# ScalarE copies the first 256 output columns of each expert tile, and issues the second expert's weight loads

## Chip, core and metric

The kernel runs on one core of a Trainium2 chip. The metric is the time of one execution on the device, in microseconds (us). It was measured three times: 692.98, 693.09 and 696.32 us, median 693.09 us. Below, PE is TensorE, DVE is VectorE, ACT is ScalarE, POOL is GpSimd and SP is SyncE; PSUM is the memory of eight banks that matmuls write to, and SBUF is the main on-chip memory.

## What is computed

Two blocks follow one another. The first is causal attention with a window of 64 positions; the second is a mixture of experts in which every token goes to one of eight experts.

```python
# attention: q, k, v are (8 batches, 8 heads, 576 positions, 64)
scores = where(0 <= i - j < 64, q @ k.T / 8, -1e9);  attn = softmax(scores) @ v
x = attn.transpose(0, 2, 1, 3).reshape(4608, 512)
# experts: w1 is (8, 512, 1024), w2 is (8, 1024, 512)
e = argmax(x @ w_gate);  g = softmax(x @ w_gate)[e]
out[n] = g[n] * (relu(x[n] @ w1[e]) @ w2[e])
```

All data is 32-bit floating point. An fp32 matmul of the program stands as two records in the trace, which is why counts of matmuls in the profile are twice those in the code.

## The kernel before

**Stages.** Until about 200 us the attention runs, head pair by head pair; its rows, scaled with the gate, are stored to `x_dram`. Meanwhile the tokens are counted per expert, and a table of slots (`perm_i`) sorts them by expert. Then the experts run, in tiles of up to 256 tokens. The rows of a tile are gathered from `x_dram` by an indirect DMA of POOL (`gather`, L282), turned by sixteen 32x32-block transposes of DVE into `xn` (`turned_blocks`, L319), copied by two instructions of ACT into `xq` (`keep_turned`, L334), multiplied, and written to their places in `out` by two indirect DMAs of POOL (`scatter`, L300), first the half `ys[1]`, then the half `ys[0]`.

**Kinds of tile.** A whole tile (256 tokens) is done with a seven-product scheme of the Strassen kind: `hidden` (L345) makes relu(x w1) in seven products of 128x128 matmuls, and `output` (L402) multiplies by w2 in seven products of 128x256 matmuls, which collect in PSUM banks 4 (`yps[0]`, halves `yx` and `yx2`), 5 (`yw`, `yy2`), 7 (`yy`) and 2 (`yw2`). The scheme needs sums of weight blocks, which POOL forms (`sums_w1`, `sums_w2`, L152 and L155, four instructions each, all of them line L142 in the profile), and sums of token blocks, which DVE forms (`sums_x`, L338, and `left_sums`, L127). An expert's last tile, if it holds 160 tokens or fewer, is a half tile (`half_tile`, L445) and, with 96 or fewer, a rest tile (`rest_tile`, L492); these use plain products. In this run there are 16 whole tiles, 3 half tiles and 2 rest tiles (L353 has 1792 records and a whole tile has 112; L479 has 48 and a half tile 16; L530 has 64 and a rest tile 32).

**The end of a tile lies in the next one.** `finish` (L434) adds the last PSUM results into `ys[0]` and `ys[1]` with DVE. It is called at the start of the following tile's `body` (L545), together with `scatter` and, at the border of two experts, with the weight sums (`between`). The first two whole tiles, called `tile0` and `tile1` here, are written out before the loop over experts (L1063 to L1122); all later ones go through `expert` (L1142).

**Order of the work.** The whole kernel stands under `manual_schedule`: each engine executes its instructions in the order in which the program text issues them. Where a generator such as `hidden` or `output` stops at a `yield`, the caller can put other work. Three orders matter here:

- In `half_tile` ACT gets, in this order, the relu of the hidden values (L463), two copies of 32x128 blocks out of bank 5 (L483, c = 0 and 2; DVE has c = 1 and 3), and then `keep_turned`, which makes the next tile's input. PE gets the L474 products (32 tokens, into bank 5) and then the L479 products (128 tokens, all 512 columns of bank 4).
- In `output` PE ends with the products `yy`, `yy2`, `yw2` and `yx2`, in this order (L422 to L431). ACT has the copy of `yx` into `y1` (L411) after the first product and `keep_turned` after the third.
- SP issues the loads of the second expert's `w1` and `w2` (2 MB each, L1133 and L1134, seen as L159 and L162 in the profile) after everything of the first two tiles; as SP has nothing else to do, it runs ahead of the other engines. The weights of the experts after it are issued from ACT's queue within a whole tile of the expert before (L1147).

The memory for the second expert's weights and sums (pool `wp`) is taken after the attention's pools (`held`: `xsp`, `small`, `rp`, and the table `hi`) have been given back.

Of the kernel before, what the change touches and what calls it, by code (L numbers as in the profile page):

```python
# [36 lines left out]
def kernel(  # L37
# [10 lines left out]
    nc = tc.nc  # L48
    P = nc.NUM_PARTITIONS
    B, H, S, D = q.shape  # L50
    NT, DM = out.shape
# [21 lines left out]
    QD = 32  # L73
# [27 lines left out]
    w1_of = lambda pool, i: pool.tile([P, NG, FF], F32, name=f"w1_{i}")  # L101
    w2_of = lambda pool, i: pool.tile([P, FT, DM], F32, name=f"w2_{i}")
# [55 lines left out]
    def load_w1(e, queue=nc.sync):  # L158
        queue.dma_start(out=w1s[e % NW][:], in_=w1v[e])  # L159

    def load_w2(e, queue=nc.sync):
        queue.dma_start(out=w2s[e % NW][:], in_=w2v[e])  # L162
# [103 lines left out]
    hs = v_m(2080, 4, HF, P)  # L266
    u3 = v_m(4128, HF, P)
    y1, v1, v3 = (v_m(4640 + n * HM, HM) for n in range(3))
    v02 = v_m(4640 + 3 * HM, DM)
    v2 = v02[:, HM:]  # L270
    xn = v_m(1024, C, NG, P)
    at_g = consts.tile([P, C], I32, name="at_g")
    at_s = consts.tile([P, C], I32, name="at_s")
# [45 lines left out]
    def turned_blocks():  # L319

        rows = xg_all.rearrange("p c (g b j) -> p c g b j", b=P // QD, j=QD)
        for a in range(P // QD):
            for b in range(P // QD):
                V.transpose(  # L324
                    out=xn[b * QD : (b + 1) * QD, :, :, a * QD : (a + 1) * QD].rearrange("p c g i -> p (c g) i"),
                    in_=rows[a * QD : (a + 1) * QD, :, :, b, :].rearrange("p c g j -> p (c g) j"),
                )
                yield
# [66 lines left out]
    def product_y(acc, a, b, start=True, stop=True):  # L395
        for f in range(HF):
            nc.tensor.matmul(  # L397
                acc, lhsT=a[:, f, :], rhs=b[:, f, :],
                start=(start and f == 0), stop=(stop and f == HF - 1), skip_group_check=True,
            )  # L400

    def output(e, blocks=None, next_x=True):  # L402

        b11, b12, b21, b22 = w2q(e)
        t = s2s[e % NW]
        a11, a12, a21, a22 = hq[:, 0, 0], hq[:, 1, 0], hq[:, 0, 1], hq[:, 1, 1]
        form(left_sums(V, hs, a11, a12, a21, a22))
        if blocks is not None:
            form_all(blocks)
        product_y(yx, a11, b11)  # L410
        nc.scalar.copy(out=y1, in_=yx)  # L411
        yield
        product_y(yw, a22, t[:, 3])
        yield
        product_y(yx, a12, b21, start=False)
        if blocks is None:
            sums_x(tps)
        elif next_x:
            keep_turned()
            sums_x([xn[:, c] for c in range(C)])  # L420
        yield
        product_y(yy, hs[:, 1], t[:, 1])  # L422
        yield
        product_y(yy2, hs[:, 2], t[:, 2])
        plus(v1, yy, y1)
        plus(v3, yy2, v1)
        V.tensor_tensor(out=ys[1][:, lo_], in0=v3, in1=yw, op=ALU.subtract)
        yield
        product_y(yw2, hs[:, 0], t[:, 0])
        yield  # L430
        product_y(yx2, hs[:, 3], b22)  # L431
        yield

    def finish():  # L434

        plus(ys[1][:, hi_], yw2, v3)
        plus(v2, yw2, v1)
        plus(ys[0], yps[0], v02)

    hp = qk_m(8192, FT, HALF)  # L440
    pps = [banks[i](0, rows_, HALF) for i, rows_ in ((0, 3), (1, 3), (6, 2))]
# [3 lines left out]
    def half_tile(e, blocks, after, next_x):  # L445

        w1, w2 = w1s[e % NW], w2s[e % NW]
        f = 0
        for n, acc in enumerate(pps):
            f0 = f  # L450
            for i in range(acc.shape[1]):
                for g in range(NG):
                    nc.tensor.matmul(
                        acc[:, i], lhsT=w1[:, g, f * P : (f + 1) * P],
                        rhs=xq[:, g].rearrange("p c s -> p (c s)")[:, 0:HALF],
                        start=(i + g == 0), stop=(g == NG - 1), skip_group_check=True,
                    )
                f += 1
            if n == 1:
                some(blocks, 8)  # L460
                V.tensor_scalar_max(hp[:, f0:f], acc, 0.0)
            else:
                relu(out=hp[:, f0:f], in_=acc)  # L463
        V.memset(v1, 0.0)
        V.memset(yw2, 0.0)
        form_all(blocks)
        if after is not None:
            gather(perm_i[:, after])

        quad = lambda c: slice(c * QD, (c + 1) * QD)  # L470
        y = y2(0, P)
        for f in range(FT):
            for c in range(NQ):
                nc.tensor.matmul(  # L474
                    y[quad(c)], lhsT=hp[:, f, P:], rhs=w2[:, f, c * P : (c + 1) * P], start=(f == 0), stop=(f == FT - 1),
                    skip_group_check=True,
                )
        for f in range(FT):
            nc.tensor.matmul(yps[0], lhsT=hp[:, f, 0:P], rhs=w2[:, f, :], start=(f == 0), stop=(f == FT - 1))  # L479
        for c in range(NQ):  # L480
            copy = V.tensor_copy if c % 2 else nc.scalar.copy
            to = ys[1] if c < NQ // 2 else v3
            copy(out=to[0:QD, c % 2 * P : (c % 2 + 1) * P], in_=y[quad(c)])  # L483
        if next_x:
            keep_turned()
            sums_x([xn[:, c] for c in range(C)])
# [5 lines left out]
    def rest_tile(e, blocks, after, next_x):  # L492

        w1, w2 = w1s[e % NW], w2s[e % NW]

        def rows(acc, tokens, ways):
            n, width = P // ways, FF // ways
            for g in range(NG):
                for c in range(ways):
                    nc.tensor.matmul(  # L500
                        acc[c * n : (c + 1) * n, 0:width], lhsT=xq[:, g, 0, tokens],
                        rhs=w1[:, g, c * width : (c + 1) * width], start=(g == 0), stop=(g == NG - 1),
                        skip_group_check=True,
                    )

        a, b = banks[0](0, FF // 2), banks[1](0, FF // 4)
        rows(b, slice(L, L + QD), 4)
        relu(out=hr4, in_=b)
        rows(a, slice(0, L), 2)
        relu(out=hr, in_=a)  # L510
        for h, t, acc in ((hr4, ht4, banks[3](0, HF // 2, P)), (hr, ht, banks[6](0, HF, P))):
            for i in range(h.shape[1] // P):
                nc.tensor.transpose(out=acc[:, i], in_=h[:, i * P : (i + 1) * P], identity=ident[:])
            nc.scalar.copy(out=t.rearrange("p i c s -> p i (c s)"), in_=acc)
        V.memset(v1, 0.0)
        V.memset(yw2, 0.0)
        form_all(blocks)
        if after is not None:
            gather(perm_i[:, after])

        y, y4 = banks[7](0, DM), y2(0, P)
        for f in range(FT):
            for c in range(4):
                nc.tensor.matmul(
                    y4[c * QD : (c + 1) * QD], lhsT=ht4[:, f % (HF // 2), f // (HF // 2)],
                    rhs=w2[:, f, c * P : (c + 1) * P], start=(f == 0), stop=(f == FT - 1), skip_group_check=True,
                )
        for f in range(FT):
            for c in range(2):
                nc.tensor.matmul(  # L530
                    y[c * L : (c + 1) * L, c * HM : (c + 1) * HM], lhsT=ht[:, f % HF, f // HF],
                    rhs=w2[:, f, c * HM : (c + 1) * HM], start=(f == 0), stop=(f == FT - 1), skip_group_check=True,
                )
        for c in range(4):
            nc.scalar.copy(out=yps[0][L : L + QD, c * P : (c + 1) * P], in_=y4[c * QD : (c + 1) * QD])
        if next_x:
            keep_turned()
            sums_x([xn[:, c] for c in range(C)])
        nc.scalar.copy(out=yps[0][0:L, hi_], in_=y[L:, hi_])
        V.tensor_copy(out=yps[0][0:L, lo_], in_=y[0:L, lo_])  # L540

    def whole_tile():
        pass
# [20 lines left out]
            ahead()  # L564
        form_all(parts)

    with tc.manual_schedule(), ExitStack() as held, ExitStack() as brief:
        xsp = held.enter_context(tc.tile_pool(name="xsp", bufs=7))
        small = held.enter_context(tc.tile_pool(name="small", bufs=4))
        rp = held.enter_context(tc.tile_pool(name="rp", bufs=2))  # L570
# [538 lines left out]
            next(table, None)  # L1109
        assert next(tile0, None) is None  # L1110
        gather(perm_i[:, 3 * C : 4 * C])
        V.memset(v02[:, lo_], 0.0)
        finish()
        scatter(perm_e[:, 0:C])
        blocks = turned_blocks()
        tile1 = chain(hidden(0), output(0, blocks))
        for _ in range(8):
            next(tile1)
        regs, end, most = loads()
        gather(perm_i[:, 4 * C : 5 * C])  # L1120
        for _ in tile1:
            pass  # L1122

    wp = ctx.enter_context(tc.tile_pool(name="wp", bufs=1))

    w1s.append(w1_of(wp, 1))
    s1s.append(s1_of(wp, 1))
    w2s.append(w2_of(wp, 1))
    s2s.append(s2_of(wp, 1))


    with tc.manual_schedule():
        load_w1(1)  # L1133
        load_w2(1)  # L1134

        def at(n):
            n = nc.s_assert_within(
# [113 lines left out]
```

## Time and profile before

| what | value |
|---|---|
| three runs | 692.98, 693.09, 696.32 us; median 693.09 us |
| the profiled execution | 693.54 us |
| its span, first to last instruction | 691.8 us |
| granted clock of PE over the span | 0.999 of full speed |
| PE busy | 669.9 us (97%) |
| weight loads of PE busy | 590.7 us (85%) |
| DVE busy | 501.5 us (72%) |
| POOL busy | 357.4 us (52%) |
| ACT busy | 263.5 us (38%) |
| DMA queues | 94.52 MB, mean 137 GB/s |

The span is what the trace covers; the execution's own time is 1.7 us longer. "PE busy" counts a matmul from its start to its modelled end; consecutive matmuls overlap, so the interval from one to the next is shorter than a matmul's own duration. In the answers of the trace a line of a timeline gives the start in us, the duration in us, the engine, the line of the code, the operation, what it writes and reads, its shape and its count, and in brackets the idle time before it with what ended that. `ACTq`, `SPq` and `POOLq` are the sequencers of these engines, which issue DMAs.

### The profile page before, as it was taken

What the parts mean: (1) busy time and instruction counts of PE and PEld (TensorE: products, weight loads), DVE (VectorE), ACT (ScalarE), POOL (GpSimd) and SP (SyncE); (2) the same over time, 40 slices, a digit from 0 to 9 for tenths busy, and PEclk for the clock granted to TensorE, in tenths of its full rate; (3) what the DMA queues carried; (4) which work ended last, traced back from release to release, by engine and by line L of the source; (5) the groups of instructions that cost most, each with busy time, mean ns of one, the idle gap of its engine ahead of it and who ended that gap; (6) DMA issues with size and microseconds to landing.
All of it is one profiled execution on the core that took longest, in us unless ns stands there. A gap on an engine that the chain in (4) does not pass through costs nothing. (4 is left out here: it accounts for less than half of the span.)

```text
span 691.8 us, 18001 instructions
## 1 busy us (share of the span) xinstructions
PE 669.9 (97%) x6894; PEld 590.7 (85%) x6894; DVE 501.5 (72%) x1646; ACT 263.5 (38%) x662; POOL 357.4 (52%) x364
## 2 busy tenths in 40 slices
PE   6999999999999999999999999999999999999996
PEld 4888888888788897997899899899689799689995
DVE  3677998898967678766776686586867486766864
ACT  5889888888855011111111121121121121121211
POOL 6414649478852208766452357356265757264012
PEclk9999999999999999999999999999999999999999
DMA  9997789988435351622601161171135161111021
GB/s 213 217 223 177 180 186 241 215 200 211 182 109 168 126 180 64 242 113 73 256 29 63 60 243 63 63 259 48 64 134 212 50 243 63 65 39 63 2 63 62
DMA packets 136767, 94.52 MB, mean 137 GB/s; under 512 B 115567, under 2 KB 115583, under 8 KB 136640
## 3 DMA queue, kind: packets, MB, share of 16 engines
q1 hardware_dynamic: 114944, 38.29, 22.2%
q0 software_dynamic: 8544, 26.50, 11.8%
q10 hardware_dynamic: 13152, 28.05, 11.6%
q8 instruction: 78, 1.28, 0.7%
q14 instruction: 49, 0.40, 0.2%
HBM read 73.94 MB, written 20.45 MB: 136 GB/s over the span
## 5 line engine op out<-in xcount | busy, mean ns | idle before, releaser
L324 DVE STREAM_TRANSPOSE v_m<-qk_m 32x256 f32<-32x256 f32 x320 | 139.3, 435 | 6.9 <-DMA qk_m<-x_dram,at_g 0.9
L285 POOL DMA_INDIRECT qk_m<-x_dram,at_g x42 | 45.4, 1080 | 164.2 <-DVE v_m L324 154.1
L353 PE MATMUL bank<-qk_m,s 128*128 128x128 f32 x1024 | 122.4, 275 | 0.0
L353 PEld LDWEIGHTS bank<-qk_m,s 128*128 128x128 f32 x1024 | 118.3, 192 | 0.0
L723 ACT ACTIVATE pr<-pr,mx 128x128 f32<-128x128 f32 x288 | 89.6, 390 | 22.0 <-DVE mx L713 21.5
L353 PE MATMUL bank<-qk_m,w 128*128 128x128 f32 x768 | 94.1, 276 | 1.0 <-PEq L1156 0.5
L353 PEld LDWEIGHTS bank<-qk_m,w 128*128 128x128 f32 x768 | 90.3, 192 | 4.7 <-issue 4.4
L713 DVE CUSTOM_DVE_ANT_0 pr<-bank,mask 128x128 f32<-128x128 f32 x288 | 64.4, 286 | 20.5 <-PE bank L700 17.7
L393 DVE TENSOR_TENSOR v_m<-bank,v_m 128x256 f32<-128x256 f32 (+1 forms) x95 | 43.8, 479 | 38.2 <-PE bank L397 27.3
L304 POOL DMA_INDIRECT out_dram<-v_m,at_s x42 | 42.5, 1011 | 54.7 <-DVE v_m L393 50.5
L142 POOL TENSOR_TENSOR s<-w 128x1024 f32<-128x1024 f32 x22 | 52.2, 2373 | 0.0
L641 POOL COPY v_m<-v_m 64x520 f32<-64x520 f32 x32 | 20.1, 627 | 61.3 <-DMA v_m<-in_v_dram 52.2
L746 PEld LDWEIGHTS bank<-v_m,pT 128*64 128x64 f32 x1152 | 40.7, 137 | 11.4 <-issue 3.9
L746 PE MATMUL bank<-v_m,pT 128*64 128x65 f32 x1152 | 47.9, 227 | 2.1 <-POOL v_m L645 0.8
L397 PE MATMUL bank<-qkT_m,v_m 128*128 128x256 f32 x216 | 48.3, 379 | 0.0
L360 ACT COPY qk_m<-bank 128x512 f32<-128x512 f32 x16 | 9.4, 587 | 99.8 <-PE bank L353 73.7
L336 ACT COPY qk_m<-v_m 128x512 f32<-128x512 f32 x40 | 22.7, 615 | 61.4 <-DVE v_m L324 61.4
L397 PEld LDWEIGHTS bank<-qkT_m,v_m 128*128 128x128 f32 x216 | 41.0, 190 | 5.5
L700 PE MATMUL bank<-qkT_m 64*64 64x128 f32 x1152 | 43.6, 281 | 0.7 <-DVE mx L713 0.7
L886 POOL TENSOR_SCALAR xs<-xs,gate 128x512 f32<-128x512 f32 x27 | 42.0, 1566 | 2.2 <-DVE gate L846 1.5
L731 PE MATMUL bank<-ident,pr 128*128 128x128 f32 x288 | 42.0, 282 | 0.0
L363 DVE TENSOR_TENSOR qk_m<-bank,qk_m 128x512 f32<-128x512 f32 x16 | 11.1, 692 | 40.7 <-PE bank L353 40.7
(197 smaller groups left out, 1247.4 us busy)
## 6 DMA issues: line engine op xcount, KB each, us to landing
w<-in_moe_w_dram ACTq DMA_DIRECT2D x9, 2048.0 KB, 8.9
qk_m<-in_q_dram SPq DMA_DIRECT2D x72, 128.0 KB, 3.5
qk_m<-in_k_dram SPq DMA_DIRECT2D x66, 128.0 KB, 3.6
v_m<-in_v_dram SPq DMA_DIRECT2D x64, 128.0 KB, 3.4
qk_m<-in_moe_w_dram ACTq DMA_DIRECT2D x3, 2048.0 KB, 11.1
w<-in_moe_w_dram SPq DMA_DIRECT2D x2, 2048.0 KB, 14.0
w<-in_moe_w_dram ACTq DMA_DIRECT2D x4, 512.0 KB, 5.0
x_dram<-xs POOLq DMA_DIRECT2D x4, 512.0 KB, 4.9
```

Of the source, the lines that this page charges most:

```text
L142: op()
L285: G.indirect_dma_start(out=xg[c], out_offset=None, in_=x_dram[:, :], in_offset=bass.IndirectOffsetOnAxis(ap=at_g[:, c : c + 1], axis=0),)
L304: put = G.indirect_dma_start(out=out[:, :], out_offset=bass.IndirectOffsetOnAxis(ap=at_s[:, c : c + 1], axis=0), in_=ys[c], in_offset=None ...
L324: V.transpose(out=xn[b * QD : (b + 1) * QD, :, :, a * QD : (a + 1) * QD].rearrange("p c g i -> p (c g) i"), in_=rows[a * QD : (a + 1) * QD ...
L353: nc.tensor.matmul(acc[:, f, :], lhsT=a[:, g, f * P : (f + 1) * P], rhs=b[:, g, :], start=(first and f == 0 and g == 0), stop=(g == HG - 1 ...
L393: plus = lambda out, a, b: V.tensor_tensor(out=out, in0=a, in1=b, op=ALU.add)
L397: nc.tensor.matmul(acc, lhsT=a[:, f, :], rhs=b[:, f, :], start=(start and f == 0), stop=(stop and f == HF - 1), skip_group_check=True,)
L700: nc.tensor.matmul(out_, lhsT=qT[rows, t, a * WINDOW : (a + 1) * WINDOW], rhs=rhs, start=True, stop=True, skip_group_check=True,)
L713: V.tensor_tensor_reduce(out=prs[h][:, m, :], in0=scs[h][:, m, :], in1=mask[:, m0 + m, :], scale=-scale, scalar=-2 * MASKED, op0=ALU.add, ...
L723: nc.scalar.activation(out=y, in_=y, func=AF.Exp, scale=-1.0, bias=mx[:, h, m : m + 1])
L731: nc.tensor.transpose(out=tr[:, m, :], in_=prs[h][:, m, :], identity=ident[:])
L746: nc.tensor.matmul(px[a * D : (a + 1) * D, h, m, :], lhsT=pTs[h][:, m, a * D : (a + 1) * D], rhs=vt[:, h, :], start=True, stop=True, skip_ ...
```

## The change

ACT, not DVE, now moves the first 256 columns of the first 128 tokens from PSUM to `ys[0]`: in `output` after the product `yy` has been issued, in `half_tile` after the L479 products. `finish` adds only the other 256 columns; `v2` no longer needs a zeroed half beside it, and the memset at L1112 goes. In `rest_tile` the copies that went to the first half of bank 4 go to `ys[0]` instead. The memory of the attention's pools is given back before `tile1`, and ACT's queue issues the loads of `w1` and `w2` of expert 1 within `tile1`, after the third and the fifth step of `hidden`; SP's two loads go.

```diff
     y1, v1, v3 = (v_m(4640 + n * HM, HM) for n in range(3))
-    v02 = v_m(4640 + 3 * HM, DM)
-    v2 = v02[:, HM:]
+    v2 = v_m(4640 + 3 * HM, HM)
...
         product_y(yy, hs[:, 1], t[:, 1])
+        nc.scalar.copy(out=ys[0][:, lo_], in_=yx)
         yield
         product_y(yy2, hs[:, 2], t[:, 2])
...
         plus(v2, yw2, v1)
-        plus(ys[0], yps[0], v02)
+        plus(ys[0][:, hi_], yx2, v2)
...
         for f in range(FT):
             nc.tensor.matmul(yps[0], lhsT=hp[:, f, 0:P], rhs=w2[:, f, :], start=(f == 0), stop=(f == FT - 1))
+        nc.scalar.copy(out=ys[0][:, lo_], in_=yx)
         for c in range(NQ):
             copy = V.tensor_copy if c % 2 else nc.scalar.copy
...
         for c in range(4):
-            nc.scalar.copy(out=yps[0][L : L + QD, c * P : (c + 1) * P], in_=y4[c * QD : (c + 1) * QD])
+            to = (ys if c < 2 else yps)[0]
+            nc.scalar.copy(out=to[L : L + QD, c * P : (c + 1) * P], in_=y4[c * QD : (c + 1) * QD])
...
         nc.scalar.copy(out=yps[0][0:L, hi_], in_=y[L:, hi_])
-        V.tensor_copy(out=yps[0][0:L, lo_], in_=y[0:L, lo_])
+        V.tensor_copy(out=ys[0][0:L, lo_], in_=y[0:L, lo_])
...
-    with tc.manual_schedule(), ExitStack() as held, ExitStack() as brief:
+    with tc.manual_schedule(), ExitStack() as brief, ExitStack() as held:
...
         gather(perm_i[:, 3 * C : 4 * C])
-        V.memset(v02[:, lo_], 0.0)
         finish()
         scatter(perm_e[:, 0:C])
         blocks = turned_blocks()
+        held.close()
+        wp = ctx.enter_context(tc.tile_pool(name="wp", bufs=1))
+        w1s.append(w1_of(wp, 1))
+        s1s.append(s1_of(wp, 1))
+        w2s.append(w2_of(wp, 1))
+        s2s.append(s2_of(wp, 1))
         tile1 = chain(hidden(0), output(0, blocks))
-        for _ in range(8):
+        for n in range(8):
             next(tile1)
+            if n in (2, 4):
+                (load_w1 if n == 2 else load_w2)(1, nc.scalar)
...
-    wp = ctx.enter_context(tc.tile_pool(name="wp", bufs=1))
-    w1s.append(w1_of(wp, 1))
-    s1s.append(s1_of(wp, 1))
-    w2s.append(w2_of(wp, 1))
-    s2s.append(s2_of(wp, 1))
     with tc.manual_schedule():
-        load_w1(1)
-        load_w2(1)
```

## The prediction

> **What bounds the kernel now.** I read the page's busy times first, then the waits, then the timelines of the places that the change touches. PE is busy in nearly every slice, and its listed waits in the expert stage come to under 4 us in all, so an instruction taken from DVE buys nothing by itself: what counts is whether PE's next matmul gets its operands, and a PSUM bank, later.
>
> ```profile
> PE 669.9 (97%) x6894; PEld 590.7 (85%) x6894; DVE 501.5 (72%) x1646; ACT 263.5 (38%) x662; POOL 357.4 (52%) x364
> PE   6999999999999999999999999999999999999996
> ```
>
> The timelines of PE, ACT and DVE at the second half tile show the place that matters. During the 7.13 us of the L479 products, ACT does its two block copies and both `keep_turned` copies (L336), DVE its two block copies and the sums of the next input (L342). So PE goes from L479 to the next tile's first product (L353, 319.94) without idling.
>
> ```profile
> 311.08 1.96 PE L474 MATMUL bank<-w,qk_m 128*32 128x128 f32 x64
> 312.97 7.13 PE L479 MATMUL bank<-w,qk_m 128*128 128x512 f32 x16
> 319.94 1.95 PE L353 MATMUL bank<-qk_m,w 128*128 128x128 f32 x16
> ...
> 313.10 0.26 ACT L483 COPY v_m<-bank 32x128 f32<-32x128 f32 x1 [1.42 <-PE bank L474]
> 314.32 0.26 ACT L483 COPY v_m<-bank 32x128 f32<-32x128 f32 x1 [0.96 <-DVE v_m L483]
> 314.48 1.13 ACT L336 COPY qk_m<-v_m 128x512 f32<-128x512 f32 x2
> ...
> 314.61 0.29 DVE L483 COPY v_m<-bank 32x128 f32<-32x128 f32 x1 [0.33 <-ACT v_m L483]
> 315.13 1.22 DVE L342 TENSOR_TENSOR qk_m<-v_m,qk_m 128x256 f32<-128x256 f32 x3 [0.23 <-ACT qk_m L336]
> ```
>
> The next lines are POOL's after the same tile, and PE's second output product, which needs POOL's last weight sum: the sum ends at 331.19 + 2.36 = 333.55, 0.62 us ahead of PE. Here PE has little cover.
>
> ```profile
> 321.75 1.02 POOL L304 DMA_INDIRECT out_dram<-v_m,at_s  x1 [4.36 <-DVE v_m L393]
> 324.08 2.40 POOL L142 TENSOR_TENSOR qkT_m<-qk_m 128x1024 f32<-128x1024 f32 x1
> 331.19 2.36 POOL L142 TENSOR_TENSOR qkT_m<-qkT_m,qk_m 128x1024 f32<-128x1024 f32 x1
> ...
> 334.17 1.89 PE L397 MATMUL bank<-qkT_m,qk_m 128*128 128x256 f32 x8
> ```
>
> In `tile1` all sixteen transposes come late, so `keep_turned` runs when PE already does `yx2` (257.73), and PE waits 0.36 us for it. In every other whole tile `keep_turned` starts about 4.3 us ahead of `yx2`.
>
> ```profile
> 257.73 1.89 PE L397 MATMUL bank<-qk_m,v_m 128*128 128x256 f32 x8
> 259.99 8.93 PE L453 MATMUL bank<-qk_m,w 128*128 128x160 f32 x64 [0.36 <-ACT qk_m L336]
> ...
> 258.70 1.14 ACT L336 COPY qk_m<-v_m 128x512 f32<-128x512 f32 x2 [8.98 <-DVE v_m L324]
> ```
>
> Last, two copies of a rest tile. They read and write disjoint elements, yet DVE, idle for 0.85 us, starts only when ACT has ended; what they share is banks. So the program orders users of a bank by the whole bank.
>
> ```profile
> 507.57 0.34 ACT L539 COPY bank<-bank 64x256 f32<-64x256 f32 x1 [1.55 <-PE bank L530]
> 507.94 0.42 DVE L540 COPY bank<-bank 64x256 f32<-64x256 f32 x1 [0.85 <-ACT bank L539]
> ```
>
> **What the Trainium skill says.** "PSUM — Partial Sum Buffer", in Engine vs sequencer instructions, calls the queues of ACT, DVE and POOL strictly FIFO; the trace agrees, as ACT's lines always stand in the program's order. The same page, in PSUM bank collisions raise a hardware error, wants PSUM guarded by bank and group of 32 partitions, not by address; the L539 and L540 pair fits. "TensorE: Matmul & The Clock Gate", Part 1, says that PE's clock can halve after an idle window of some 3.4 us; no gap of the expert stage in this trace is that long, and the clock is 0.999. I use it for the upper end alone.
>
> **Part 1: the copy in the half tile.** It stands in ACT's queue ahead of the two L483 copies and of `keep_turned`, and it needs the end of L479. Behind the waiting copy stand those four ACT instructions; for them wait DVE's L483 and L342, and PE's next tile. Everything that lay beside the 7.13 us of L479 comes after it. Worked on the tile above:
> - L479 ends at 312.97 + 7.13 = 320.10. A reader starts 0.10 later, as ACT does after L453 (311.15 to 311.25): 320.20.
> - The new copy is a 128x256 one out of PSUM, like L411 with 0.37; ACT's next starts 0.10 before its end (as L336 does after L483): 320.47.
> - Block c = 0, 0.26: 320.73. DVE's c = 1 starts 0.03 later and takes 0.28: 321.04. ACT's c = 2 starts 0.04 later: 321.08 to 321.34. The trace of before shows this alternation of ACT and DVE in all three half tiles.
> - `keep_turned` c = 0 from 321.24, half of a pair that takes 1.13 to 1.14, 0.61 alone: 321.85. PE follows its releaser by 0.15 (259.84 to 259.99 in `tile1`): 322.00.
> PE started at 319.94, so it loses 2.06 us. The first product needs no more than c = 0; DVE's first two sums are ready 0.85 us later, under the first product's 1.79. Three half tiles, each followed directly by a whole one: **6.2 us**. Bounds: 1.6 each if the blocks don't alternate (without 0.28, 0.07 and some hand-over), 2.6 if PE waits for both copies of `keep_turned`.
>
> **Part 2: the weight sums behind it.** DVE now has its four sums in 321.89 to 323.45 and begins `finish` at 323.55, not 320.50. POOL's first scatter follows the start of `finish` by 1.25 (320.50 to 321.75), so 324.80; both take 2.33 with the gap until the sums, which start at 327.13 and take 9.47 (324.08 to 333.55): 336.60. PE, now 2.06 late, wants the last sum at 334.17 + 2.06 = 336.23. With 0.1 for the hand-over it waits 0.45 us. The other two half tiles come to the same sum, since there too the scatters wait for `finish`. Three times: **1.35 us**; bounds 0 and 0.8 each.
>
> **Part 3: the copy in the whole tile.** 0.37 us of ACT per tile, beside PE. Its place is behind `keep_turned`; in the usual tile (338.51 to 339.65, so the copy ends at 339.92) bank 4 is free 2.9 us before `yx2` (342.81): nothing. In `tile0` ACT is idle at that time: nothing. In `tile1` the copy runs from 259.74 to 260.11, and `yx2` writes the same bank: by the order by bank it starts at 260.26 rather than 257.73. It takes 1.73 to the next tile, which starts at 261.99 instead of 259.99 (the old wait of 0.36 vanishes in it): **2.0 us**, once. Bounds: 0 if elements count and not banks, else 2.0. I take 2.0 because of L539 and L540.
>
> **Part 4: what DVE saves.** The last addition of `finish` becomes 0.42 instead of 0.69; the memset of 0.27 goes. Within the tiles PE waits for neither. At the very end it shows:
>
> ```profile
> 685.67 0.69 DVE L393 TENSOR_TENSOR v_m<-bank,v_m 128x512 f32<-128x512 f32 x1 [0.97 <-PE bank L397]
> 686.64 1.00 POOL L304 DMA_INDIRECT out_dram<-v_m,at_s  x1 [0.42 <-POOLq L1214]
> ```
>
> DVE would end at 686.09. The last scatter is then bound by the one before it (ends at 686.22, and pairs of scatters lie 0.30 apart): 686.52 for 686.64, so **-0.1 us**, at most -0.27.
>
> **Part 5: the loads.** SP issued them at 234.98 and 235.40. ACT issues them after L367 and L376 of `tile1`, at about 241.1 and 245.4; each issue takes 0.37 of ACT's sequencer (L159 and L162 elsewhere), and ACT is idle for 3 us after each. What they wait for, the table's last matmul, ended before 235. The pair took 14.0 us to landing (median); from 245.4 that is 259.4. The first reader is POOL's sum at 265.79: over 6 us of cover. Without it PE would lose at most what a load is late. The gather issued at 236.26 is freed of their traffic, but its rows are transposed only from 251.50: nothing. They are ahead of POOL's next gather (259.46) in time as before, and end at about that point, so that gather isn't slowed. The rest tile's copies change place and not order: nothing.
>
> **Sum.** 6.2 + 1.35 + 2.0 - 0.1 = 9.4 us. Against the profiled execution's 693.54 that is 702.9; that execution is 0.45 above the median of the runs, and I put the 9.4 on the median 693.09: **702.5 us**.
>
> **The rivals.**
> - First stall alone (chance 0.13): POOL's slack or `tile1`'s bank order doesn't bite. 693.1 + 6.1 = 699.2 with neither; 700.5 without the bank order alone. For it: the 0.45 of part 2 is a difference of long sums. Against: L539 and L540.
> - Longer stalls (0.2): PE waits for both `keep_turned` copies, or POOL for more: 3 x 0.5 + 3 x 0.35 more gives 705.0; a halved clock for one window of 3.4 us after each stall would add up to 1.7 each, but the stalls are shorter than the window.
> - Not slower (0.09): ACT's stream isn't the program's, and the half tile's copy lies behind `keep_turned`. Then the three stalls and part 2 vanish, and if `tile1` is free too, the tail's 0.1 is left: 693.0. The point that decides: whether ACT's first L483 copy of a half tile starts before or after the end of L479. The trace speaks against it.
> - Faster (0.03): DVE's 0.27 per tile would have to be on PE's path. PE's whole idle time in the expert stage bounds this at 3.6 us, 689.5; no listed wait of PE there is for `finish`.
>
> The forecast itself has 0.55. About 0.5% is what a measurement of this kernel can tell from no change. The range, 699.0 to 705.0, takes in the first two rivals; what lies outside is the third and fourth and part of the second's clock case. Slower by over 0.5% (above 696.6): 0.88; within: 0.09; faster: 0.03.
>
> **What would show it.** Right: ACT's new copy at L479's end and both L483 copies after it; a PE gap of about 2 us ahead of L353 after each half tile, put down to ACT's L336; one of about 0.4 us ahead of the second L397 product, put down to POOL; a gap of 2.5 us ahead of `yx2` in `tile1`; L159 and L162 once more on ACT at 241 and 245 and none on SP. Wrong: no gap after the half tiles, or loads that land after 265 and hold POOL's sums.

## The result, and the profile after

The kernel became slower: 711.41 us (median of six runs, 708.59 to 715.06) against 695.45 us for the kernel before in the same comparison (six runs), a ratio of 1.0248 with a 95% interval of 1.0225 to 1.0271. The forecast of slower by stalls of PE held; its size, 702.5 us in a range of 699.0 to 705.0, did not. The profiled execution took 709.95 us, 16.4 more than the 693.54 of before; the spans differ by 16.3.

First the busy times on the page of the changed kernel. PE is busy for 3.7 us more (673.6 us), in a span that is longer by 16.3; so most of the added time is time in which PE stands idle. DVE is relieved by 2.9 us.

```profile
PE 673.6 (95%) x6894; PEld 591.6 (84%) x6894; DVE 498.6 (70%) x1645; ACT 268.7 (38%) x681; POOL 358.4 (51%) x364
```

PE's waits in the changed kernel, each line with the sum in us, the number of waits and the longest. Line numbers have shifted, and every view below has those of the run that it shows: L352 is `hidden`'s product, L335 `keep_turned`, L396 `output`'s product, L422 the new copy in `output`, L142 POOL's weight sums, L362 DVE's first addition in `hidden`, which uses what PE's product before it left in PSUM. None of these waits stands among PE's in the kernel before.

```profile
PE bank L352 <- ACT qk_m L335: 5.2, 3, 1.7
PE bank L396 <- POOL qkT_m L142: 3.7, 2, 1.9
PE bank L396 <- ACT v_m L422: 2.3, 1, 2.3
PE bank L352 <- DVE qk_m L362: 0.9, 2, 0.5
PE bank L396 <- POOL s L142: 0.3, 1, 0.3
```

The second half tile again, PE, ACT and DVE. ACT stands idle for 8.45 us before its new copy (L480), until L479 has ended; then come its block copies (L484) and `keep_turned`, and only then PE's next tile: the order that the prediction laid out. DVE ends its sums (L341) at 329.52 and begins `finish` (L392) only at 331.94, which the prediction did not lay out.

```profile
319.11 7.13 PE L479 MATMUL bank<-w,qk_m 128*128 128x512 f32 x16
327.98 2.05 PE L352 MATMUL bank<-qk_m,w 128*128 128x128 f32 x16 [1.73 <-ACT qk_m L335]
...
326.28 0.37 ACT L480 COPY v_m<-bank 128x256 f32<-128x256 f32 x1 [8.45 <-PE bank L479]
327.31 1.13 ACT L335 COPY qk_m<-v_m 128x512 f32<-128x512 f32 x2
...
329.10 0.42 DVE L341 TENSOR_TENSOR qk_m<-qk_m,v_m 128x256 f32<-128x256 f32 x1
331.94 0.76 DVE L392 TENSOR_TENSOR v_m<-bank,v_m 128x256 f32<-128x256 f32 x2 [2.42 <-PE bank L352]
```

POOL's scatter, which waits for `finish`, and its weight sums then follow late, and PE waits for the last of these sums before its second output product (L396):

```profile
333.18 1.02 POOL L303 DMA_INDIRECT out_dram<-v_m,at_s  x1 [9.80 <-DVE v_m L392]
342.61 2.35 POOL L142 TENSOR_TENSOR qkT_m<-qkT_m,qk_m 128x1024 f32<-128x1024 f32 x1
...
345.01 1.35 PE L396 MATMUL bank<-qkT_m,qk_m 128*128 128x256 f32 x5 [1.85 <-POOL qkT_m L142]
```

In `tile1` `yx2` waits for the new copy, at the predicted place. But then its eight records take 2.99 us instead of 1.89. The second view below has two stretches: start, end and length, the busy time of PE, PEld, DVE, ACT and POOL (with the number of instructions), then PE's granted clock. PE is busy for 1.15 us of the first stretch, which holds the gap, and in the second stretch the granted clock is 0.50.

```profile
260.14 2.99 PE L396 MATMUL bank<-qk_m,v_m 128*128 128x256 f32 x8 [2.27 <-ACT v_m L422]
...
259.72 0.36 ACT L422 COPY v_m<-bank 128x256 f32<-128x256 f32 x1
```

```profile
257.57:260.99 3.42, 1.15 (x6) 0.77 (x5) 2.68 (x8) 1.41 (x3) 1.25 (x2) 1.00 0.00 0
260.99:264.40 3.41, 3.41 (x12) 2.97 (x11) 2.25 (x6) 0.00 (x0) 2.10 (x3) 0.50 0.58 154
```

PE executes the same 6894 records in both traces, so each one's start can be set against its counterpart, and the difference is PE's delay. It grows at these places and hardly elsewhere (the predicted growth is that of the prediction's parts 3, 1 and 2, from top to bottom):

| place | delay before it, us | delay after it, us | predicted growth | measured growth |
|---|---|---|---|---|
| `tile1`, `yx2` to the end of the slow stretch | -0.02 | 3.59 | 2.0 | 3.6 |
| three half tiles, start of the next tile | | | 3 x 2.06 | 3 x 1.90 |
| first half tile, to the second output product | 5.49 | 6.04 | 0.45 | 0.55 |
| second half tile, the same | 8.04 | 10.84 | 0.45 | 2.80 |
| third half tile, the same | 13.06 | 15.92 | 0.45 | 2.86 |
| last product | | 16.26 | 9.55 | 16.3 |

The rest, some 0.7 us, is scattered in steps of 0.1 to 0.3.

### The profile page after: what moved, and what is told of

Read it like the earlier page. It is cut to its first block, busy times and chain, and to the rows that moved or that the text cites. A ratio compares the mean times of both kernels' runs of the same rounds, so it can differ in the third digit from the quotient of the medians.

```text
span 708.1 us, 18050 instructions
## 1 busy us (share of the span) xinstructions
PE 673.6 (95%) x6894; PEld 591.6 (84%) x6894; DVE 498.6 (70%) x1645; ACT 268.7 (38%) x681; POOL 358.4 (51%) x364
## 5 line engine op out<-in xcount | busy, mean ns | idle before, releaser
L352 PE MATMUL bank<-qk_m,s 128*128 128x128 f32 x1024 | 122.6, 275 | 0.9 <-DVE qk_m L362 0.9
L352 PEld LDWEIGHTS bank<-qk_m,s 128*128 128x128 f32 x1024 | 118.3, 192 | 1.3 <-issue 1.3
L352 PE MATMUL bank<-qk_m,w 128*128 128x128 f32 x768 | 94.3, 276 | 6.1 <-ACT qk_m L335 5.2
L352 PEld LDWEIGHTS bank<-qk_m,w 128*128 128x128 f32 x768 | 90.2, 192 | 10.4 <-ACT qk_m L335 7.7
L392 DVE TENSOR_TENSOR v_m<-bank,v_m 128x256 f32<-128x256 f32 x95 | 38.2, 421 | 39.4 <-PE bank L396 28.9
L142 POOL TENSOR_TENSOR s<-w 128x1024 f32<-128x1024 f32 x22 | 52.2, 2375 | 0.0
L396 PE MATMUL bank<-qkT_m,v_m 128*128 128x256 f32 x216 | 48.3, 379 | 0.0
L335 ACT COPY qk_m<-v_m 128x512 f32<-128x512 f32 x40 | 22.7, 615 | 65.8 <-DVE v_m L323 65.7
L396 PEld LDWEIGHTS bank<-qkT_m,v_m 128*128 128x128 f32 x216 | 41.0, 190 | 5.5
L669 PE MATMUL bank<-ident,qk_m 128*128 128x128 f32 x256 | 35.2, 282 | 7.5 <-DMA qk_m<-in_q_dram 6.4
```

Of the source, the lines that this page charges most:

```text
L142: op()
L352: nc.tensor.matmul(acc[:, f, :], lhsT=a[:, g, f * P : (f + 1) * P], rhs=b[:, g, :], start=(first and f == 0 and g == 0), stop=(g == HG - 1 ...
L396: nc.tensor.matmul(acc, lhsT=a[:, f, :], rhs=b[:, f, :], start=(start and f == 0), stop=(stop and f == HF - 1), skip_group_check=True,)
```

## The experiments

All differences are against the kernel before, measured beside it on the same chip; the differences in us are worked out from the ratio of the times, those in brackets from its interval. Theory A: the two places of the new copy in ACT's queue, with what follows from them, are the whole cost. The others, B to G, are named in the expectations.

**Half tile's copy behind `keep_turned`** (label e1_half_late).

```diff
-        nc.scalar.copy(out=ys[0][:, lo_], in_=yx)
         for c in range(NQ):
...
             keep_turned()
             sums_x([xn[:, c] for c in range(C)])
+        nc.scalar.copy(out=ys[0][:, lo_], in_=yx)
```

> The changed kernel with one edit undone: in the half tile ACT's copy of the first 256 columns stands behind the block copies and keep_turned, not ahead of them. Theory A (two places of the new copy in ACT's queue): the three PE gaps of 1.9 us after the half tiles go, and with them PE's later waits for POOL's weight sums (0.5, 2.8 and 2.9 us); what is left is the 3.6 us of tile1 (a gap of 2.4 us ahead of the last output product and about 1.5 us at a lower clock after it). So 3.6 us, about 0.5%, above the kernel before, 12.5 us below the changed one. Rival B (the moved loads and the earlier return of the memory cost the time): still 10 us or more above the kernel before.

Measured: 698.39 us (8 runs) against 694.24, ratio 1.0045 [1.0028, 1.0062], so 3.1 us more (1.9 to 4.3), and about 13 less than the changed kernel. PE's gaps after the half tiles and its waits for POOL are gone; the wait for the copy in `tile1` stands alone, as PE's waits show. This time the clock stays at 1.00 in both stretches that the gap touches and in the one after them (264.70 to 268.11, not shown), so the gap alone costs 2.0 us of PE's delay.

```profile
PE bank L396 <- ACT v_m L422: 2.3, 1, 2.3
```

```profile
257.88:261.29 3.41, 2.45 (x12) 1.81 (x10) 3.13 (x8) 0.15 (x1) 0.00 (x0) 1.00 0.00 1
261.29:264.70 3.41, 2.10 (x11) 1.90 (x11) 2.74 (x8) 1.25 (x3) 2.38 (x3) 1.00 0.21 52
```

**The whole tile's copy ahead of `keep_turned`** (label e2_whole_early).

```diff
         product_y(yx, a12, b21, start=False)
+        nc.scalar.copy(out=ys[0][:, lo_], in_=yx)
...
         product_y(yy, hs[:, 1], t[:, 1])
-        nc.scalar.copy(out=ys[0][:, lo_], in_=yx)
```

> The changed kernel with another edit: in output the copy stands directly behind the third product, ahead of keep_turned in ACT's queue; the half tile's copy stays first. Theory A: in tile1 the copy runs some 6 us before PE needs bank 4, so the gap of 2.4 us and the slow matmuls behind it go; the three half tiles keep their cost. 12 to 12.6 us above the kernel before. Rival B: as the changed kernel, 16 us above. Rival C (the clock drop in tile1 isn't from the gap but chance): the gap goes and some slow matmuls stay.

Measured: 707.23 us (6 runs), ratio 1.0171 [1.0147, 1.0195], 11.9 us more. `tile1` has no gap and no slow stretch; the time is against rival B, while rival C can't be told from a single trace without the gap (part 3 below returns to it). The sum fits by its size, but not by its parts: in this trace the third half tile costs 2.4 us and not 4.8, the stretch behind the second one's wait for POOL runs at a lower clock (1.7 us), and PE waits 1.39 and 1.30 us shortly after the start of the two rest tiles, which the changed kernel doesn't. At the third half tile DVE begins `finish` 0.11 us after its sums, with no wait, and what PE loses behind it is 0.51 us, not the 2.86 of the changed kernel, although the half tile's own instructions are the same:

```profile
564.24 0.42 DVE L341 TENSOR_TENSOR qk_m<-qk_m,v_m 128x256 f32<-128x256 f32 x1
564.77 0.75 DVE L392 TENSOR_TENSOR v_m<-bank,v_m 128x256 f32<-128x256 f32 x2
```

**Both edits** (label e3_both).

> Both edits: the half tile's copy behind keep_turned, the whole tile's copy ahead of it; loads on ACT and the shorter additions of DVE as in the changed kernel. Theory A: all gaps go, so within 0.5 us of the kernel before, with the last scatter about 0.1 us earlier. Rival B: 4 us or more above the kernel before, since the moved loads are still there.

Measured: 696.48 us (22 runs), ratio 1.0040 [1.0025, 1.0055], 2.8 us more (1.7 to 3.8). All gaps of theory A are gone, yet the time isn't that of the kernel before. Its trace shows what is left: PE starts each rest tile, executes 30 or 32 records and stops for 1.25 and 1.61 us, put down to "issue", that is, to no other engine.

```profile
492.74 1.93 PE L501 MATMUL bank<-w,qk_m 128*32 128x256 f32 x30 [0.17 <-issue]
495.91 4.20 PE L501 MATMUL bank<-w,qk_m 128*32 128x256 f32 x18 [1.25 <-issue]
```

**The moved loads alone, on the kernel before** (label e4_loads_only). The edit is the change's last hunk: memory returned before `tile1`, two loads on ACT.

> The kernel before with one part of the change: the memory is returned before tile1 and ACT issues the loads of the second expert's weights within tile1; DVE still adds all 512 columns. Theory A: nothing, within 0.5 us of the kernel before, loads landed by about 258 us and POOL's first weight sum at about 266 as before. Rival B: several us slower.

Measured: 694.93 us (14 runs) against 694.24, ratio 0.9999 [0.9986, 1.0013]: nothing. In its trace POOL's first weight sum starts at 266.42, 1.00 after its second scatter's issue as before, so no load holds it. Rival B falls. One line of this trace matters below. Its half tile is that of the kernel before, and at the second one DVE stands idle for 2.99 us before `finish` (L393) with no releaser, and begins it 0.42 us before L479 has ended (320.73):

```profile
320.31 0.76 DVE L393 TENSOR_TENSOR v_m<-bank,v_m 128x256 f32<-128x256 f32 x2 [2.99 <-issue]
```

**DVE set free of the copy in the half tile** (label e5_half_dve).

```diff
-            copy = V.tensor_copy if c % 2 else nc.scalar.copy
+            copy = V.tensor_copy
...
             keep_turned()
-            sums_x([xn[:, c] for c in range(C)])
+            sums_xn()
```

`sums_xn` is `sums_x`, reading `xn` where that reads its copy `xq`.

> The changed kernel with the half tile's new copy still first in ACT's queue, but with DVE set free of it: DVE does all four block copies, and its sums of the next input read xn, the source of keep_turned, and not its result. Theory A (behind the half tile DVE stands at a jump and gets its next instructions late, up to 2.9 us after the branch, because its work now ends right before it): DVE reaches the branch some 3 us before L479 ends, finish starts about 0.4 us after L479 ends, as in the kernel before, and POOL's last weight sum no longer holds PE; the gap after each half tile shrinks from 1.9 to about 1.25 us, since the copy and the first half of keep_turned are still in line. In sum 8 us above the kernel before, 8 below the changed one. Rival D (finish really waits for PE's second product of the next tile, as the profile names it): finish still starts at the end of that product, some 3.6 us after the first one begins, and PE still waits about 2 us for POOL at two of the three half tiles; 12 us or more above the kernel before.

Measured: 701.64 us (6 runs) against 694.77, ratio 1.0096 [1.0069, 1.0123], so 6.7 us more (4.8 to 8.5), and about 10 less than the changed kernel. PE's delay grows by 1.14 at each half tile, a little under the 1.25 expected, and no wait for POOL is left. The second half tile of this kernel (L486 is the 128-token product, L348 the sums, L399 `finish`) shows why:

```profile
318.42 7.13 PE L486 MATMUL bank<-w,qk_m 128*128 128x512 f32 x16
326.53 2.05 PE L359 MATMUL bank<-qk_m,w 128*128 128x128 f32 x16 [0.98 <-ACT qk_m L335]
...
321.91 0.41 DVE L348 TENSOR_TENSOR qk_m<-qk_m,v_m 128x256 f32<-128x256 f32 x1
325.18 0.76 DVE L399 TENSOR_TENSOR v_m<-bank,v_m 128x256 f32<-128x256 f32 x2 [2.86 <-issue]
```

`finish` starts at 325.18, before L486 has ended (325.55) and before the next tile's first product: it waits for no product of the next tile, so rival D falls. Yet DVE stood idle for 2.86 us with nothing to wait for. The place is the end of the half tile's arm, where the program branches over the code of the other arms to the next expert's tile. In the kernel before the same idle stretch of DVE, from 316.69 to 320.50, ended 0.40 us after L479, and the profile put it down to PE.

**The early copy in `tile1` alone, the half tile's copy behind `keep_turned`** (label e6_tile1_early). `output` gets a flag for the place of its copy, which `tile1` alone sets.

> The changed kernel with the half tile's copy behind keep_turned and with the early copy of the whole tile in tile1 alone, the other whole tiles as in the change. It tells whether the 2.2 us that the kernel with both edits kept (1.6 us of PE waiting for its own instructions at the start of each of the two rest tiles) belong to the copy's place in the loop's whole tiles. Theory E (they do, or they hang on how the program is laid out in memory): no such wait here, and the time is within 1 us of the kernel before. Rival F (they are the price of the shorter additions of DVE or of the moved loads): again 2 us above.

Measured: 695.23 us (22 runs) against 694.77, ratio 1.0007 [0.9995, 1.0019]. Level with the kernel before: no gap after a half tile, no wait for the new copy in `tile1`, no stop above 0.3 us in a rest tile. It holds the shorter additions of DVE and the moved loads, so rival F falls, and it shows what those are worth: nothing that can be measured.

**The kernel with both edits once more** (label e7_both_again).

> The kernel with both edits once more, for a second profile. If the waits of 1.6 us at the start of the two rest tiles belong to this program, they stand again in this trace; if they are chance of a single execution, one or both are missing.

Measured: one run, 694.72 us, with the stops at the same places, 1.30 and 1.89 us. So they aren't the chance of one execution. They stand in the three traces with the early copy in every whole tile (e2, e3, e7), and in no other trace does PE stop for more than 0.6 us there. PE's instructions are the same, in the same order, as in the changed kernel; what differs is where the program lies in memory and what the other engines do. Which of the two it is wasn't tried.

**The half tile's part by itself** (label e8_half_first): the early copy in `tile1` alone, the half tile's copy first in ACT's queue.

> The changed kernel with the early copy in tile1 alone; the half tile's copy stays first in ACT's queue. It is the half tile's part by itself, without tile1's gap and, if they belong to the layout of the kernel with the early copy everywhere, without the waits at the start of the rest tiles. Theory A: three gaps of 1.9 us, 0.5 us of waiting for POOL at the first half tile and 2.8 us at each of the others where the jump's wait of DVE is exposed (0.5 where it isn't): 7 to 12 us above the kernel before, most likely 11 to 12. Rival G (the parts aren't additive: the gaps after the half tiles cost less once tile1 is free): under 6 us.

Measured: 709.32 us (5 runs) against 694.23, ratio 1.0204 [1.0173, 1.0235], so 14.2 us more (12.0 to 16.3): above theory A's range of 7 to 12, and far from rival G. PE's delay grows by the expected steps (three of 1.90 to 1.95; 0.55, 3.0 and 2.7 behind them). What was not in the sum is the clock behind the second half tile's wait for POOL, 0.50 in the stretch after it, which costs 1.7 us; about 1.5 us more are scattered:

```profile
340.36:343.77 3.41, 1.54 (x8) 1.04 (x7) 3.14 (x2) 0.57 (x2) 2.95 (x3) 1.00 1.00 381
343.77:347.18 3.41, 3.41 (x10) 2.70 (x9) 3.17 (x7) 0.13 (x1) 0.00 (x0) 0.50 0.48 182
```

## Why the prediction was right in its kind and wrong in its size

**Part 1, the copy in the half tile: right.** The chain of ACT's copy, the alternating block copies and `keep_turned` stands in the trace as written; 1.90 us each instead of 2.06. With the copy behind `keep_turned` (e1) the gaps are gone, with DVE free of it (e5) they shrink to the part that is ACT's own.

**Part 2, the weight sums behind it: the step that failed.** The prediction put "the start of `finish`" at 0.10 us after DVE's sums: "DVE now has its four sums in 321.89 to 323.45 and begins `finish` at 323.55". At the first half tile that held (0.13 us, and PE's loss there is 0.55 for 0.45), as it did at the third half tile of e2 (0.11 us, 0.51). At the second and third half tile of the changed kernel `finish` began 2.4 us after the sums. So POOL's sums came that much later, and PE lost 2.80 and 2.86 us: it waited about 0.5 us for DVE (L362), and then 1.85 and 1.87 us for POOL. The loss goes with the late start of `finish`: in e5, where `finish` begins before L479's end, it is 0.11 us or less, and at the third half tile of e2 it has the predicted size.

What holds DVE there? I had read DVE's 3.82 us of idle time at the second half tile of before (first line below) as waiting for L479, as the profile puts it down. e4 and e5 contradict this reading: there DVE stands idle for 2.99 and 2.86 us with no releaser, and goes on before L479 has ended. So DVE is held at the end of the half tile's arm by something of its own, and at the second half tile it was hidden under L479 in the kernel before. The change moved DVE's work behind L479, right up to the end of the arm, and so uncovered it. At the third half tile this explains less: there the kernel before shows a wait of 0.38 us only (second line, before), and the changed kernel one of 2.46 (third line, changed).

```profile
320.50 0.76 DVE L393 TENSOR_TENSOR v_m<-bank,v_m 128x256 f32<-128x256 f32 x2 [3.82 <-PE bank L479]
546.85 0.75 DVE L393 TENSOR_TENSOR v_m<-bank,v_m 128x256 f32<-128x256 f32 x2 [0.38 <-DMA out_dram<-v_m,at_s]
566.79 0.76 DVE L392 TENSOR_TENSOR v_m<-bank,v_m 128x256 f32<-128x256 f32 x2 [2.46 <-PE bank L352]
```

Over all ten traces DVE stands idle before `finish` for 2.38 to 3.82 us at the second half tile in every one, at the third for 2.35 to 3.01 us in five (changed, e1, e5, e6, e8) and for 0.38 us or less in the other five, and at the first for no more than 0.14 us. e3 and e7, one program, agree in this. That DVE waits for its instructions to arrive after the branch is a likely reading, since the wait stands at a branch, mostly without a releaser where nothing else ends near it, and changes with the program; but no run isolated it, and the cause of the wait stays open.

**Part 3, `tile1`: right in place and wait, short by the clock.** The order by bank, read off two copies of the rest tile, was borne out: ACT reads 256 columns of bank 4, PE writes the other 256, and PE waited 2.27 us. Without a change of clock the loss is the predicted 2.0 us (e1); in the changed kernel's profile it is 3.6, since the clock fell to half for 3.41 us. The Trainium skill, "TensorE: Matmul & The Clock Gate", Part 1, gives an idle window of some 3.4 us for this, and the prediction kept the case outside its range because "the stalls are shorter than the window". Here the measurement differs and decides: gaps of 1.87 to 2.27 us were followed by the lower clock in some traces and not in others. The records of the clock show what sorts them. From the first record of the full clock on, every change to half lies a whole multiple of 3.413 us after it (in the changed kernel 249.17 us, 73 times; in e2 331.09, 97 times; in e8 334.51, 98 times), so an execution is divided into stretches of 3.41 us. With PE's idle time summed up in each stretch:

| trace | stretch from, us | PE idle in it, us | clock in the next |
|---|---|---|---|
| e5 (in the attention) | 16.08 | 2.66 | 0.50 |
| changed | 257.57 | 2.27 | 0.50 |
| e2 | 339.88 | 1.89 | 0.50 |
| e8 | 340.36 | 1.87 | 0.50 |
| changed | 342.90 | 1.85 | 1.00 |
| e2 | 322.81 | 1.78 | 1.00 |
| e1 | 257.88 and 261.29 | 0.97 and 1.30 | 1.00 |

No stretch of the ten traces goes against this order: with 1.87 us or more the next one is at half the clock, with 1.85 or less at the full one. (So close to the limit the figures are no surer than the modelled ends of the matmuls.) The same gap of 2.27 us lay within one stretch in the changed kernel and across two in e1. So the slow matmuls of `tile1` do come from the gap, against rival C, but a gap of this length brings them only where most of it lies in one stretch. Where the stretches lie differs from one execution to the next, so this part of the time is chance, and the range should have held it. Of the six runs of the changed kernel the two shortest (708.59 and 709.06 us) show a mean clock of 0.998, the two longest (714.91 and 715.06 us) one of 0.991.

**Parts 4 and 5: right.** The last scatter starts 1.32 us after the start of PE's last record, not 1.44, which is the 0.1 us of the tail; the moved loads cost nothing (e4), and DVE's shorter additions bring nothing that can be measured (e6).

**The sum.** 6.2 became 5.7; 1.35 became 6.2; 2.0 became 3.6; with some 0.7 scattered, 16.3 for 9.4. Of the missing 6.9 us, 4.9 lie in part 2, nearly all behind DVE's wait at the end of the arm, and 1.6 are the clock. The bound of "0.8 each" for part 2 left out what DVE may need between its sums and `finish`. The trace of before gave a sign of it, at one of three places: the idle time there is 0.10 us at the first half tile, 3.82 at the second and 0.38 at the third.

The rivals: of the first (POOL's slack or the order by bank doesn't bite) nothing held. The second (longer stalls) came true in two of its points, the waits for POOL and the halved clock, but with more than the 0.35 us that it gave POOL, and with the clock that it had put aside. The third fell at the point named, as ACT's first L484 copy starts after L479's end, and the fourth with the measured time.

## What to carry to other kernels

A copy that waits for the last product of a stage is not free on an idle engine: what counts is what stands behind it in that engine's queue. Here its place in the half tile alone, ahead of or behind two block copies and two input copies, decides over some 13 us, and e6, with the new copies put where they hold up nothing that PE waits for, is as fast as before. Read a wait that ends with the bottleneck engine with suspicion: it can hide a second wait that shows as soon as the first is moved. And count a stall of the bottleneck engine not by its length alone but with what late engines do after it, and with what a fall of the clock may add.

## What the runs showed of the hardware

- PE's clock fell to half after every stretch of 3.41 us in which PE had been idle for 1.87 us or more, and in none of the ten traces after a stretch with 1.85 us or less; ahead of the end of the program it came back after 3.41 us. In the expert stage this happened in three traces (changed, e2, e8) and cost 1.6 to 1.8 us each time.
- At the end of the half tile's arm DVE stood idle for 2.35 to 3.82 us before its next instruction in 15 of 30 cases, always at the second half tile, never at the first. PE stopped for 1.25 to 1.89 us shortly after entering each rest tile in the three traces with the early copy in every whole tile (e2, e3, e7), and for at most 0.6 us in the others, with the same PE instructions.
- A read by ACT and a write by PE to different columns of one PSUM bank were kept apart in time by the program: PE waited 2.27 us for a copy of 0.36, which stood behind `keep_turned` in ACT's queue.
